# Second layer of the last phase with weights stationary for five of six blocks, its sums turned by VectorE in squares of 32

## The chip, the core and the metric

The kernel runs on one core of a Trainium2 chip. The core has five engines that work side by side and wait for each other by semaphores: TensorE (matmuls), VectorE, ScalarE, GpSimd and SyncE, which here issues all DMA transfers. The metric is the time of one execution on the device in microseconds (us), less is better; several runs give a median.

## What is computed

Three parts follow each other: a gated linear attention, a mixture of four experts, and a feed-forward layer with a gate. Cut to what matters here:

```python
def _moe2_ref(x, w_in, w_out):        # x: 3072 x 384, w_in: 384 x 2048, w_out: 2048 x 384
    h = x @ w_in
    relu6 = np.clip(h + 3.0, 0.0, 6.0)
    g = h * relu6 / 6.0
    return (g @ w_out).astype(np.float32)

def reference(...):
    x = attention(q, k, v, alpha)     # 3072 tokens of 384 features
    x = sum over 4 experts of p[e] * (relu(x @ w1[e]) @ w2[e])   # 384 x 1024, 1024 x 384
    return _moe2_ref(x, w_in, w_out)  # stored as 3072 rows of 384
```

## The kernel before

The 3072 tokens are split in six blocks of 512 (`NBLK` = 6, `NB` = 512). Activations lie with the features on the 128 partitions and the tokens in the free dimension, so 384 features are three tiles (`KT` = 3). Hidden units are taken 128 at a time; one such piece of a block is a step. The function walks through phases 0, 1 and 2: phases 0 and 1 are the experts (`kind` 1), phase 2 is the last layer (`kind` 2). A visit is one block with one set of weights; in phase 2 a block is one visit of 16 steps.

Each value is split in a high part and a low part (`xh`, `xl`; `wh`, `wl`; `hh`, `hl`), and each product is made of three matmuls: high by high, low weights by high, high weights by low.

A step has two halves. `mm1` (line 778) makes the first layer: nine matmuls into one PSUM bank `ph`, 128 hidden units by 512 tokens, weights stationary. In phase 2 four operations follow it, alternating between the engines: ScalarE makes `g` (L812), VectorE multiplies it by `ph` (L815), ScalarE makes `hh` (L816), VectorE makes `hl` (L817). `mm2` (line 822) makes the second layer. In `kind` 1 the weights are stationary and 512 columns of activations move (L849), into three sums `po`, each 128 features by 512 tokens. In `kind` 2 the activations are stationary and 384 columns of weights move (L851), into four sums, each 128 tokens by 384 features. `finish` (line 881) takes a sum that is complete: in `kind` 2 ScalarE copies it to `o` (L902) and SP stores it (L904), 128 rows of 1536 bytes.

`mm2` runs one step behind `mm1`, across blocks too: TensorE does the first layer of a block's step 0, the second layer of the last step of the block before, the first layer of step 1, and only then the second layer of step 0. PE, VectorE, ScalarE and SP work in the order in which the code is written (`tc.manual_schedule`, line 907). So what `finish` issues stands on its engine behind the four operations of the next block's step 0 and in front of those of step 1.

The sums have a pool `ps2` of three banks (and one bank of `ps1` for a fourth sum), so in phase 2 each sum of a block takes the bank that the same sum of the block before had. The pool `gp` holds the tags "pb" and "t" with two buffers each; the pool `sp` holds "acc", also two buffers, which `o` uses. Of the DMA transfers that are spoken of below, `vd` (L137) copies 256 tokens of 8 heads of `v` in DRAM, 2048 pieces of 48 numbers (192 bytes), and one call of `A` (L493) writes 768 pieces of 512 bytes with four transfers.

Of the kernel before, what the change touches and what calls it, by code (L numbers as in the profile page):

```python
# [10 lines left out]
F32 = mybir.dt.float32  # L11
# [7 lines left out]
P = 128  # L19
# [522 lines left out]
def tile_gla__then__moe__then__moe2(  # L542
# [29 lines left out]
    nc = tc.nc  # L572
# [4 lines left out]
    KT = DM // P  # L577
    NB = 512
    NBLK = N // NB
# [13 lines left out]
    gp = ctx.enter_context(tc.tile_pool(name="gp", bufs=2))  # L593
# [228 lines left out]
    def mm2(vi, f):  # L822
        vv = visits[vi]
        i, z = vv["steps"][f]
        wh, wl = wts[(1, i)]
        hh, hl = hts.pop((vi, f))
        n = vv["n"]
        first, last = f == 0, f == len(vv["steps"]) - 1
        nt = KT if vv["kind"] == 1 else n // P
        half = n < NB  # L830
        if first and half:
            po = [psh.tile([P, 2, U], F32, tag="psh", name=f"po_{vi}_{x}") for x in range(2)]
            accs[vi] = [po[0][:, 0], po[0][:, 1], po[1][:, 0]]
        elif first:
            nonlocal ps2
            if ps2 is None:
                ps_ctx.close()
                ps2 = ctx.enter_context(tc.tile_pool(name="ps2", bufs=3, space=PSUM, reuse_waits="tile"))
            second = vv["phase"] == 1 and vi % 2
            pools = [(psa, "psa") if second else (ps2, "ps2") if m < 3 else (ps1, "ps1") for m in range(nt)]  # L840
            accs[vi] = [pool.tile([P, 512], F32, tag=tag, name=f"po_{vi}_{m}") for m, (pool, tag) in enumerate(pools)]
        for m in range(nt):
            ms = slice(m * P, m * P + P)
            for o, (w, h) in enumerate(((wh, hh), (wl, hh), (wh, hl))):
                fl = dict(start=(first and o == 0 and not (half and m == 1)), stop=(last and o == 2))
                if half:
                    fl["skip_group_check"] = True
                if vv["kind"] == 1:
                    pe.matmul(accs[vi][m][:, 0:n], w[:, z, ms], h[:, 0:n], **fl)  # L849
                else:  # L850
                    pe.matmul(accs[vi][m][:, 0:DM], h[:, ms], w[:, z, :], **fl)  # L851
            if last and (m > 0 or not half):
                for x in (0, 1) if half and m == 1 else (m,):
                    finish(vi, x)
# [26 lines left out]
    def finish(vi, m):  # L881
        vv = visits[vi]
        po = accs[vi][m]
        n = vv["n"]
        b, t0 = vv["b"], vv["b"] * NB + vv["lo"]
        if vv["kind"] == 1:
            pb = pbs[vi][:, 0:n]
            if vv["phase"] == 0 and m == KT - 1:
                t = pbs[vi]
            else:  # L890
                t = gp.tile([P, 512], F32, tag="t", name=f"t_{vi}_{m}")
            nc.vector.tensor_tensor(t[:, 0:n], po[:, 0:n], pb, op=mul)  # L892
            if vv["phase"] == 0:
                after(2, lambda: nc.sync.dma_start(acc_d[vv["e"]][:, m, t0 : t0 + n], t[:, 0:n]))
                return
            a = acc[b][:, m, :]
            nc.vector.tensor_tensor(a, a, t, op=add)
            if vv["steps"][-1] == (S1 - 1, 1):
                after(1, lambda: nc.sync.dma_start(x2_d[:, m, t0 : t0 + n], a))
        else:  # L900
            o = sp.tile([P, KT, NB], F32, tag="acc", name=f"o_{vi}_{m}")[:, 0, 0:DM]
            nc.scalar.copy(o, po[:, 0:DM])  # L902
            r0 = b * NB + m * P
            nc.sync.dma_start(out[r0 : r0 + P, :], o)  # L904
# [80 lines left out]
    def after(n, fn):  # L985
        todo.append((step + n, fn))
# [36 lines left out]
    for vi, vv in enumerate(visits):  # L1023
        phase, b = vv["phase"], vv["b"]
# [15 lines left out]
        for f in range(len(vv["steps"])):  # L1040
# [12 lines left out]
            if done:  # L1053
                mm2(*done)
# [15 lines left out]
            i, z = v2["steps"][done[1]]  # L1070
# [11 lines left out]
            if i == (0, S0, S1)[v2["phase"]] + 2 and (v2["phase"] > 0 or v2["b"] == NBLK - 1):  # L1082
                ph, nb = (v2["phase"], v2["b"] + 1) if v2["b"] + 1 < NBLK else (v2["phase"] + 1, 0)
                if ph <= 2:
                    n = 2 * nb + z
# [6 lines left out]
    for x in pend:  # L1092
        mm2(*x)
# [30 lines left out]
```

## Time and profile before

| | |
|---|---|
| median of 3 runs | 1415.39 us |
| the three runs | 1412.38, 1415.39, 1415.56 us |
| profiled execution, from first to last instruction | 1412.8 us |
| TensorE busy with matmuls | 1375.2 us, 97% |
| VectorE, ScalarE busy | 840.3 us, 461.1 us |
| mean granted TensorE clock | 0.991 of full speed |

The profile is of one execution. PE is TensorE, PEld its loading of stationary operands, DVE is VectorE, ACT ScalarE, SPq the queue of SyncE. Matmuls are pipelined: one that lasts 0.39 us may be followed by the next 0.23 us after its start, so work is measured from start to start. A note `[0.18 <-ACT o L902]` says that the engine sat idle for 0.18 us before the instruction and what ended that; without a note there was no idle time that the profile shows. The last phase begins at about 1004 us.

### The profile page before, as it was taken

The page shows a single profiled execution, that of the slowest core. Times are in us where ns is not written, and L with a number is a line of the kernel's source. Part 1 is how long each engine was busy: PE and PEld are TensorE (multiplying, and loading weights), DVE is VectorE, ACT ScalarE, POOL GpSimd, SP SyncE. Part 2 cuts the span into 40 slices and gives each one's busy share as a digit, 9 for nine tenths or more (in the row PEclk, how much of TensorE's full clock was granted, in tenths as well). Part 3 has the DMA queues.
Part 4 walks back from the last instruction along what each step waited for, and adds up shares of the span by engine and source line. Part 5 has one row for each costly group of instructions (what it writes and reads, how often), then busy time and mean ns, then how long its engine had stood idle before and what let it go on. Part 6 is the DMA issues. An engine that isn't in the chain of part 4 may idle for free.

```text
span 1412.8 us, 26163 instructions
## 1 busy us (share of the span) xinstructions
PE 1375.2 (97%) x10914; PEld 1176.5 (83%) x10914; DVE 840.3 (59%) x1509; ACT 461.1 (33%) x839; POOL 91.8 (6%) x125
## 2 busy tenths in 40 slices
PE   8689999999999999999999999999999999999998
PEld 7678878888888878888888888888899999998987
DVE  7999877767685268757576666445433333333332
ACT  3555444443434133211111111113333333333333
POOL 2000000000000012222122121000000000000000
PEclk9999999999999999999999999999999999999999
DMA  6654544344532256424142424123201010101000
GB/s 192 180 151 130 154 128 133 103 114 126 143 109 87 65 186 224 149 61 151 54 138 75 138 70 140 29 93 112 78 1 45 1 45 0 45 0 46 0 23 23
DMA packets 127749, 132.33 MB, mean 94 GB/s; under 512 B 33680, under 2 KB 109456, under 8 KB 127632
## 3 DMA queue, kind: packets, MB, share of 16 engines
q1 hardware_dynamic: 127632, 130.68, 30.6%
q8 instruction: 85, 1.39, 0.4%
q14 instruction: 32, 0.26, 0.1%
HBM read 100.71 MB, written 34.65 MB: 96 GB/s over the span
## 4 chain that ended last, share of the span: by engine, by line
PE 87%; DVE 9%; issue 1%; DMA 1%; ACT 1%; SPq 0%; POOL 0%; DVEq 0%; ACTq 0%; POOLq 0%
PE ph L796 40%; PE po L849 25%; PE po L851 14%; PE py L458 2%; PE py L479 1%; PE pa L368 1%; DVE qt L356 1%; PE pkt L321 1%; DVE kt L356 1%; PE pu L404 1%; DVE asb L380 1%; DVE hl L807 1%; PE idle L938 1%; DVE dg L247 1%; PE pqt L321 1%
## 5 line engine op out<-in xcount | busy, mean ns | idle before, releaser
L804 ACT ACTIVATE hh<-ph 128x512 fp32r<-128x512 f32 (+1 forms) x206 | 117.5, 571 | 524.6 <-PE ph L796 524.5
L807 DVE SCALAR_TENSOR_TENSOR hl<-ph,hh 128x512 fp32r<-128x512 f32 (+1 forms) x206 | 134.4, 653 | 241.9 <-ACT hh L804 241.9
L796 PE MATMUL ph<-xh,w0h 128*128 128x512 f32 (+1 forms) x906 | 257.5, 393 | 2.7 <-ACT xh L771 2.4
L796 PE MATMUL ph<-xh,w0l 128*128 128x512 f32 (+1 forms) x906 | 248.4, 383 | 0.0
L796 PE MATMUL ph<-xl,w0h 128*128 128x512 f32 (+1 forms) x906 | 247.7, 382 | 0.2 <-DVE xl L772 0.2
L849 PE MATMUL po<-hl,w1h 128*128 128x512 f32 (+1 forms) x618 | 232.5, 376 | 7.3 <-DVE hl L807 7.3
L849 PE MATMUL po<-hh,w1h 128*128 128x512 f32 (+1 forms) x618 | 232.2, 376 | 6.7 <-DVE t L892 6.5
L849 PE MATMUL po<-hh,w1l 128*128 128x512 f32 (+1 forms) x618 | 231.7, 375 | 0.0
L796 PEld LDWEIGHTS ph<-xh,w0l 128*128 128x128 f32 x906 | 168.0, 190 | 34.5
L796 PEld LDWEIGHTS ph<-xl,w0h 128*128 128x128 f32 x906 | 167.3, 189 | 34.3 <-DVE xl L772 0.5
L796 PEld LDWEIGHTS ph<-xh,w0h 128*128 128x128 f32 x906 | 162.4, 190 | 28.0 <-ACT xh L771 2.6
L815 DVE SCALAR_TENSOR_TENSOR g<-g,ph 128x512 f32<-128x512 f32 x96 | 66.1, 689 | 190.9 <-ACT g L812 190.9
L849 PEld LDWEIGHTS po<-hl,w1h 128*128 128x128 f32 x618 | 116.4, 188 | 29.6 <-DVE hl L807 8.6
L849 PEld LDWEIGHTS po<-hh,w1h 128*128 128x128 f32 x618 | 116.5, 189 | 29.2 <-issue 2.9
L849 PEld LDWEIGHTS po<-hh,w1l 128*128 128x128 f32 x618 | 116.4, 188 | 20.6
L851 PE MATMUL po<-w1h,hh 128*128 128x384 f32 x384 | 130.1, 339 | 1.8 <-ACT hh L816 1.7
L851 PE MATMUL po<-w1h,hl 128*128 128x384 f32 x384 | 129.8, 338 | 0.2
L851 PE MATMUL po<-w1l,hh 128*128 128x384 f32 x384 | 129.0, 336 | 0.0
L812 ACT ACTIVATE g<-ph,three 128x512 f32<-128x512 f32 x96 | 66.2, 690 | 178.0 <-PE ph L796 178.0
L817 DVE SCALAR_TENSOR_TENSOR hl<-g,hh 128x512 fp32r<-128x512 f32 x96 | 66.6, 693 | 67.1 <-ACT hh L816 67.1
L816 ACT ACTIVATE hh<-g 128x512 fp32r<-128x512 f32 x96 | 60.8, 633 | 76.2 <-DVE g L815 76.2
L851 PEld LDWEIGHTS po<-w1h,hh 128*128 128x128 f32 x384 | 72.1, 188 | 7.8 <-ACT hh L816 2.5
(105 smaller groups left out, 1428.7 us busy)
## 6 DMA issues: line engine op xcount, KB each, us to landing
rx<-x_d SPq DMA_DIRECT2D x36, 384.0 KB
vl<-vd SPq DMA_DIRECT2D x96, 96.0 KB
rw<-in_moe_w_dram SPq DMA_DIRECT2D x21, 384.0 KB
pb<-p_d SPq DMA_DIRECT2D x28, 256.0 KB
raw<-in_moe_w_in_dram SPq DMA_DIRECT2D x24, 256.0 KB
raw<-in_moe_w_out_dram SPq DMA_DIRECT2D x24, 256.0 KB
acc_d<-t SPq DMA_DIRECT2D x20, 256.0 KB
rq<-in_q_dram SPq DMA_DIRECT2D x24, 192.0 KB
```

The costliest lines, as they stand in the source:

```text
L321: pe.transpose(pt[:, P * i : P * i + P], src[:, 4 * half + i].rearrange("p h d -> p (h d)"), self.ident)
L356: tt(zv, zv, tlv[:, :, 1 - x].unsqueeze(2).to_broadcast([P, nb, w]), op=mul)
L458: pe.matmul(s["py"][j][64 * h : 64 * h + 64, r, :].rearrange("p (b x w) -> p b x w", x=2, w=w)[:, :, 1, :], self.vl[64 * j : 64 * j + 64, ...
L796: pe.matmul(ph[:, 0:n], w[:, j, fs], x[:, j, cs], start=(o == 0 and j == 0), stop=(o == 2 and j == KT - 1),)
L804: nc.scalar.activation(hh[:, 0:n], ph[:, 0:n], AF.Relu)
L807: nc.vector.scalar_tensor_tensor(hl[:, 0:n], ph[:, 0:n], 0.0, hh[:, 0:n].bitcast(F32), op0=ALU.max, op1=sub)
L812: nc.scalar.activation(g[:, 0:n], ph[:, 0:n], AF.Relu, bias=three)
L815: nc.vector.scalar_tensor_tensor(g[:, 0:n], g[:, 0:n], 6.0, ph[:, 0:n], op0=ALU.min, op1=mul)
L816: nc.scalar.activation(hh[:, 0:n], g[:, 0:n], AF.Copy, scale=1.0 / 6.0)
L817: nc.vector.scalar_tensor_tensor(hl[:, 0:n], g[:, 0:n], 1.0 / 6.0, hh[:, 0:n].bitcast(F32), op0=mul, op1=sub)
L849: pe.matmul(accs[vi][m][:, 0:n], w[:, z, ms], h[:, 0:n], **fl)
L851: pe.matmul(accs[vi][m][:, 0:DM], h[:, ms], w[:, z, :], **fl)
```

## The change

For blocks 0 to 4 of the last phase `mm2` takes the form that phases 0 and 1 have: weights stationary, 512 tokens moving, three sums of 128 features by 512 tokens. The result then lies with the features on the partitions, while it is stored by rows of tokens. `finish` lets VectorE transpose each sum in squares of 32 by 32 into a tile of tag "t" of the pool `gp`, and SP stores it with four transfers, one for 32 partitions each: 512 pieces of 32 numbers (128 bytes) per transfer. Block 5 keeps the old form.

```diff
@@ mm2
-        nt = KT if vv["kind"] == 1 else n // P
+        wide = vv["kind"] == 1 or vv["b"] < NBLK - 1
+        nt = KT if wide else n // P
...
-                if vv["kind"] == 1:
+                if wide:
                     pe.matmul(accs[vi][m][:, 0:n], w[:, z, ms], h[:, 0:n], **fl)
                 else:
                     pe.matmul(accs[vi][m][:, 0:DM], h[:, ms], w[:, z, :], **fl)
@@ finish
+        elif b < NBLK - 1:
+            o = gp.tile([P, 512], F32, tag="t", name=f"o_{vi}_{m}")
+            nc.vector.transpose(o, po)
+            dst = out[b * NB : b * NB + NB, m * P : m * P + P].rearrange("(x j) (a i) -> a j x i", j=32, i=32)
+            for a in range(P // 32):
+                nc.sync.dma_start(dst[a], o[32 * a : 32 * a + 32].rearrange("j (x i) -> j x i", i=32))
         else:
             o = sp.tile([P, KT, NB], F32, tag="acc", name=f"o_{vi}_{m}")[:, 0, 0:DM]
             nc.scalar.copy(o, po[:, 0:DM])
```

The order of the instructions moves at each of the five block boundaries. VectorE, from block 0 to block 1, before (names are tiles of the program with a running number; `DMAHW5` and the like are the semaphores on which transfers report their landing):

```order
L815 SCALAR_TENSOR_TENSOR g_15_11598<-g_15_11598,ph_15_11586 128x512 [waits Activation_49]
L817 SCALAR_TENSOR_TENSOR hl_15_11597<-g_15_11598,hh_15_11596 128x512 [waits PE_49,Activation_49]
L815 SCALAR_TENSOR_TENSOR g_0_11627<-g_0_11627,ph_0_11615 128x512 [waits Activation_49]
L817 SCALAR_TENSOR_TENSOR hl_0_11626<-g_0_11627,hh_0_11625 128x512 [waits PE_49,Activation_49]
L815 SCALAR_TENSOR_TENSOR g_1_11668<-g_1_11668,ph_1_11656 128x512 [waits Activation_49]
L817 SCALAR_TENSOR_TENSOR hl_1_11667<-g_1_11668,hh_1_11666 128x512 [waits PE_49,Activation_49]
```

The same place in the changed kernel:

```order
L815 SCALAR_TENSOR_TENSOR g_0_11581<-g_0_11581,ph_0_11569 128x512 [waits Activation_49]
L817 SCALAR_TENSOR_TENSOR hl_0_11580<-g_0_11581,hh_0_11579 128x512 [waits PE_49,Activation_49]
L903 STREAM_TRANSPOSE o_0_11589<-po_0_11183 128x512 [waits PE_49]
L903 STREAM_TRANSPOSE o_1_11598<-po_1_11184 128x512 [waits PE_49]
L903 STREAM_TRANSPOSE o_2_11607<-po_2_11185 128x512 [waits DMAHW5_49,DMAHW6_49,DMAHW4_49,DMAHW7_49,DVE_49,PE_49]
L815 SCALAR_TENSOR_TENSOR g_1_11625<-g_1_11625,ph_1_11613 128x512 [waits Activation_49]
L817 SCALAR_TENSOR_TENSOR hl_1_11624<-g_1_11625,hh_1_11623 128x512 [waits Activation_49]
```

Three transposes now stand between step 0 and step 1 of the next block, and the third waits on the semaphores of transfers. In the boundaries that follow, the first two carry waits on transfers of the block before as well.

TensorE, the second layer of block 1's step 0, before:

```order
L796 MATMUL ph_1_11656<-xl_1_11378,w0h_10713 128x512 x3
L851 MATMUL po_0_11673<-w1h_10717,hh_0_11625 128x384 [waits Activation_49]
L851 MATMUL po_0_11673<-w1l_10718,hh_0_11625 128x384
L851 MATMUL po_0_11673<-w1h_10717,hl_0_11626 128x384 [waits DVE_49]
L851 MATMUL po_1_11674<-w1h_10717,hh_0_11625 128x384 [waits Activation_49]
L851 MATMUL po_1_11674<-w1l_10718,hh_0_11625 128x384
L851 MATMUL po_1_11674<-w1h_10717,hl_0_11626 128x384
L851 MATMUL po_2_11675<-w1h_10717,hh_0_11625 128x384 [waits Activation_49]
```

and in the changed kernel:

```order
L796 MATMUL ph_1_11613<-xl_1_11356,w0h_10713 128x512 x3
L850 MATMUL po_0_11630<-hh_0_11579,w1h_10717 128x512 [waits DVE_49,Activation_49]
L850 MATMUL po_0_11630<-hh_0_11579,w1l_10718 128x512
L850 MATMUL po_0_11630<-hl_0_11580,w1h_10717 128x512
L850 MATMUL po_1_11631<-hh_0_11579,w1h_10717 128x512 [waits DVE_49]
L850 MATMUL po_1_11631<-hh_0_11579,w1l_10718 128x512
L850 MATMUL po_1_11631<-hl_0_11580,w1h_10717 128x512
L850 MATMUL po_2_11632<-hh_0_11579,w1h_10717 128x512 [waits DVE_49]
```

The first matmul into each sum waited for ScalarE's copies; it now waits for VectorE's transposes. Nine matmuls stand per step in place of twelve.

SP's stores of block 0, in the changed kernel (before, four rows of 128x384 stand here):

```order
L906 DMA out_dram<-o_0_11589 32x16x32 [waits DVE_49]
L906 DMA out_dram<-o_0_11589 32x16x32
L906 DMA out_dram<-o_0_11589 32x16x32 [waits DMAHW6_49]
L906 DMA out_dram<-o_0_11589 32x16x32 [waits DMAHW7_49]
L906 DMA out_dram<-o_1_11598 32x16x32 [waits DMAHW0_49,DVE_49]
L906 DMA out_dram<-o_1_11598 32x16x32 [waits DMAHW1_49]
```

Six more of this kind follow for `o_1` and `o_2`.

## Rows read from the trace of the kernel before

**Rows 1.** The page, busy time of each engine

```profile
PE 1375.2 (97%) x10914; PEld 1176.5 (83%) x10914; DVE 840.3 (59%) x1509; ACT 461.1 (33%) x839; POOL 91.8 (6%) x125
```

**Rows 2.** Timeline, TensorE, wide steps: start us, us, engine, line, operation, tiles, form, count

```profile
1000.11 0.84 PE L796 MATMUL ph<-xh,w0h 128*128 128x512 f32 x3
...
1002.15 0.39 PE L849 MATMUL po<-hh,w1h 128*128 128x512 f32 x1
...
1004.19 0.84 PE L796 MATMUL ph<-xh,w0h 128*128 128x512 f32 x3
```

**Rows 3.** Timeline, TensorE, a step of the last phase

```profile
1396.39 0.86 PE L796 MATMUL ph<-xh,w0h 128*128 128x512 f32 x3
...
1398.47 0.33 PE L851 MATMUL po<-w1h,hh 128*128 128x384 f32 x1
...
1400.57 0.86 PE L796 MATMUL ph<-xh,w0h 128*128 128x512 f32 x3
```

**Rows 4.** Timeline, all engines, from block 0 to block 1

```profile
1071.32 0.33 PE L851 MATMUL po<-w1h,hh 128*128 128x384 f32 x1
...
1073.69 0.69 DVE L817 SCALAR_TENSOR_TENSOR hl<-g,hh 128x512 fp32r<-128x512 f32 x1 [0.70 <-ACT hh L816]
...
1074.05 3.60 SPq L904 DMA_DIRECT2D out_dram<-o  x4
...
1076.06 0.99 ACT L902 COPY o<-po 128x384 f32<-128x384 f32 x2 [1.65 <-DMA out_dram<-o]
...
1076.59 0.19 PEld L851 LDWEIGHTS po<-w1h,hh 128*128 128x128 f32 x1 [0.18 <-ACT o L902]
```

**Rows 5.** Timeline, SP queue, stores of blocks 4 and 5

```profile
1342.47 67.62 SPq L904 DMA_DIRECT2D out_dram<-o  x8
```

**Rows 6.** Groups by line, 900 to 1413 us: count, busy us, mean ns, idle

```profile
L892 DVE TENSOR_TENSOR t<-po,pb 128x512 f32<-128x512 f32 x13 | 8.9, 683 | 0.0
```

**Rows 7.** Timeline, SP queue, writes and copies in small pieces

```profile
414.17 0.60 SPq L137 DMA_DIRECT2D vd<-in_v_dram  x1
...
476.59 1.83 SPq L493 DMA_DIRECT2D x_d<-ys  x4
...
480.30 0.37 SPq L762 DMA_DIRECT2D rx<-x_d  x1
```

**Rows 8.** Busy time by stretch, around the copy into vd

```profile
core 0: us, PE busy (x) PEld busy (x) DVE busy (x) ACT busy (x) POOL busy (x), PEclk, DMA share, GB/s
...
418.00:419.00 1.00, 1.00 (x48) 0.88 (x39) 1.00 (x2) 0.00 (x0) 0.00 (x0) 1.00 0.44 59
419.00:420.00 1.00, 1.00 (x68) 1.00 (x64) 0.86 (x3) 0.00 (x0) 0.00 (x0) 1.00 0.00 0
```

**Rows 9.** Busy time by stretch, while block 0 is stored

```profile
1075.00:1075.50 0.50, 0.50 (x3) 0.38 (x3) 0.00 (x0) 0.00 (x0) 0.00 (x0) 1.00 1.02 366
```

**Rows 10.** Timeline, TensorE, behind a wait for VectorE in phase 0

```profile
505.99 0.47 PE L849 MATMUL po<-hh,w1h 128*128 128x512 f32 x1 [1.98 <-DVE t L892]
...
507.94 0.63 PE L849 MATMUL po<-hh,w1l 128*128 128x512 f32 x1
508.37 0.63 PE L849 MATMUL po<-hl,w1h 128*128 128x512 f32 x1
```

**Rows 11.** Busy time by stretch, at idle times and behind them

```profile
94.00:96.60 2.60, 0.00 (x0) 0.00 (x0) 2.47 (x4) 1.97 (x4) 0.00 (x0) 1.00 0.67 154
...
97.80:101.10 3.30, 3.30 (x43) 3.00 (x42) 3.23 (x6) 1.87 (x3) 0.00 (x0) 0.50 0.78 239
...
158.10:159.90 1.80, 0.02 (x1) 0.01 (x1) 1.66 (x5) 0.57 (x2) 0.00 (x0) 1.00 0.58 125
159.90:163.30 3.40, 3.38 (x53) 3.19 (x54) 3.37 (x6) 1.28 (x3) 0.00 (x0) 1.00 0.79 239
...
504.00:506.00 2.00, 0.02 (x2) 0.04 (x1) 1.93 (x5) 1.95 (x4) 0.61 (x1) 1.00 0.00 0
...
507.40:510.70 3.30, 3.30 (x9) 2.62 (x9) 3.23 (x6) 0.00 (x0) 1.38 (x1) 0.50 0.44 162
```

## The prediction, made before the changed kernel was run

> **What bounds the kernel now.** I read the busy shares first, then the timeline of TensorE's matmuls, then what stands around a block boundary. TensorE is busy for 97% of the span, VectorE for 59% [rows 1]: the end is set by the matmuls, so an edit pays only by shorter matmul work or costs by making TensorE wait.
>
> The timeline shows two kinds of step. In a step of the phase before, which the changed blocks copy, nine matmuls of the first layer start at 1000.11, nine of the second (weights stationary, 512 columns) at 1002.15, and the next step starts at 1004.19: 2.04 + 2.04 = 4.08 us [rows 2]. In a step of the last phase the first layer starts at 1396.39, twelve matmuls of 384 columns at 1398.47, the next step at 1400.57: 2.08 + 2.10 = 4.18 us [rows 3]. Both forms move 4608 columns in the second layer, yet the wide one is shorter, and the first layer behind it too.
>
> The boundary between blocks 0 and 1 comes next [rows 4]. The last second-layer visit of block 0 begins at 1071.32; call that T0. VectorE's hl for the next block ends at 1073.69 + 0.69 = T0 + 3.06, ScalarE has copied the first sum by 1074.05, where SP issues its transfer. ScalarE's third copy then waits 1.65 us until that transfer has landed, at 1076.06, because o has two buffers; TensorE loses 0.18 us on it. This is the wait to watch: it is there already, on an engine with time to spare.
>
> **The steps.** Blocks 0 to 4 have 16 steps each. A block's period, boundary included, is (1342.47 - 1074.05) / 4 = 67.1 us [rows 4, 5]. Sixteen wide steps take 16 x 4.08 = 65.3 us. That is 1.8 us saved per block, 9.1 us in five. Block 5 keeps the narrow form.
>
> One rule speaks against this gain. The Trainium skill's page "TensorE: Matmul & The Clock Gate", section "Back-to-back issue gap", gives a warm matmul N / 2.4 ns plus 2.5 ns. By it, nine of 512 and twelve of 384 differ by 7.5 ns, an estimate of 0.6 us in 80 steps, and the sum below would end some 8 us higher. The trace disagrees, with 2.04 against 2.10 us for the two sets [rows 2, 3], and the measured rows decide.
>
> **What leaves and what comes at a boundary.** Four copies leave ScalarE, which waits for TensorE anyway: worth nothing in itself. Three transposes come to VectorE, and twelve transfers to SP in place of four. The trace has no transpose. The nearest row is VectorE's product of a sum in PSUM, 128 by 512, at 0.683 us [rows 6]; I take 0.69 us. It has one source less but turns squares, so 0.5 to 1.2 us are the ends I keep; each 0.1 us moves the stall below by 0.2 us, since the first and the third transpose both lie on its path.
>
> In the changed order VectorE has the transposes behind hl of the next block's step 0 and in front of g of its step 1. The third one carries waits on four transfer semaphores, those of the first one's four transfers, since the tag "t" has two buffers. The wait that ScalarE bears now thus moves into VectorE's queue, and it is longer, because the buffer is free only when four transfers have landed. Queued behind it on VectorE are g and hl of step 1. In front of TensorE stands the first matmul into the third sum, which reuses the bank that this transpose reads.
>
> **How long the four transfers take.** SP issues the first at T0 + 3.06 + 0.69 = T0 + 3.75. Let L be the time from there to the landing of the fourth. If the small pieces cost nothing, L is three issues and one landing: four similar writes (x_d from ys, 512-byte pieces) are issued in 1.83 us, 0.46 each [rows 7], and a 192 KB transfer lands 2.0 us after its issue [rows 4]: 3 x 0.46 + 2.0 = 3.4 us. Four such x_d writes of 768 pieces have landed by 480.30, when the load that reads them is issued, 3.7 us after the first issue [rows 7]. The nearest row in number and size of pieces is the copy of v into vd: 2048 pieces of 192 bytes, the same 2048 that four of the new transfers have at 128 bytes. It is issued at 414.17 [rows 7], and the DMA engines, still busy for 0.44 of the stretch from 418 to 419, move nothing in the next [rows 8]: some 4.3 us, with another load's tail in front. I take 3.9 us, between these. The upper end is a piece that costs as much as one of 1536 bytes: 366 GB/s over 16 engines is 67 ns each [rows 9], so 128 x 67 ns = 8.6 us, and with the 1.45 us of latency in the row of 2.0 us, L = 10.
>
> **The stall.** The third transpose starts at T0 + 3.75 + L, ends 0.69 later, and TensorE starts some 0.05 behind (1076.06 + 0.48 for a copy, then 1076.59 [rows 4]): T0 + 4.49 + L. TensorE wants that bank at T0 + 2.04 (this visit) + 2.04 (first layer of step 1) + 2 x 0.68 (first two sums) = T0 + 5.44. The stall is L - 0.95: 2.95 us with L = 3.9, 2.45 with 3.4, 9 with 10. The first two sums are free in time: transposes 0 and 1 end at T0 + 3.75 and + 4.44, wanted at + 4.08 and + 4.76. After the stall g, hh and hl of step 1 need about 2.1 us from the transpose's end, and TensorE has 0.68 + 2.04 us of work until it wants them, so no second wait follows.
>
> **The clock.** Where TensorE waited 1.98 us for VectorE between wide matmuls [rows 10], the granted clock was 0.50, the 1.2 GHz level, from 507.4 to 510.7 [rows 11]: matmuls started 0.43 us apart (507.94, 508.37) instead of 2.04 / 9 = 0.227 [rows 2, 10]. After 2.6 us of idle at 94.0 the clock was 0.50 from 97.8 to 101.1; after 1.80 us of idle at 158.1 it stayed at 1.00 [rows 11]. A stall of 2.95 us is longer than either idle time that cost the clock. Price: in 3.4 us at the low level 3.4 x (1 - 0.227 / 0.43) = 1.6 us are lost.
>
> **Sum.** Per boundary 2.95 + 1.6 = 4.55 us; five boundaries 22.75 us; less 9.1 us saved: +13.65 us. Against the profiled execution that is 1412.8 + 13.65 = 1426.4 us. The median of the three runs, 1415.39, lies 2.6 us above that span, so on the median I predict 1429 us, 1.0% slower. What a measurement of this kernel can tell from no change is about 0.3%, or 4.2 us.
>
> **Rivals.** (a) The stall comes, but the clock holds, as after the 1.80 us: 5 x 2.95 - 9.1 = +5.65, 1421 us. For it: one idle time of 1.80 us in this trace kept the clock. Against it: 1.98 and 2.6 us did not.
>
> (b) The stall is short and the clock holds: L at its lower end of 3.4, 5 x 2.45 - 9.1 = +3.15, 1418.5 us, within the 0.3%. It needs pieces of 128 bytes that cost nothing beyond a plain landing.
>
> (c) Small pieces are slow. At 366 GB/s over 16 engines [rows 9] 512 bytes take 22 ns; a write that reads and writes 512 bytes for each 128-byte piece takes twice that, 45 ns, so 128 x 45 ns + 1.45 us = 7.2 us for L, a stall of 6.25, and 5 x (6.25 + 1.6) - 9.1 = +30, 1446 us. The vd row speaks against it: 4.3 us x 16 / 2048 is at most 34 ns a piece [rows 7, 8]. The Trainium skill's page "DMA: Bandwidth & Descriptors", section "Specifications", states such a rule: below 512 bytes the engine does a read-modify-write. By that rule (c) holds; the vd row doesn't bear it out in full.
>
> (d) The other sign: the transfers land inside the cover, the steps' 9.1 us remain, 1406 us at best. It decides at a stall plus clock of (9.1 - 4.2) / 5 = 0.98 us per boundary, that is at L = 1.93 us. The shortest landing here is 2.0 us for one transfer alone [rows 4], and this wait is for four in a row from one queue. It would need the four to be issued far faster than 0.46 us apiece.
>
> That the change doesn't do what it says can be left out: the order shows three sums of 512 columns per step in blocks 0 to 4 and five times three transposes.
>
> **Chances.** The forecast with stall and clock 0.62, (a) 0.16, (b) 0.10, (c) 0.08, (d) 0.04. Faster by over 0.3% is (d), 0.04. Within 0.3% is (b) and a small part of (a), 0.12. Slower is the rest, 0.84. The range runs from 1418, the lower end of (b), to 1446, which takes in (c); what is left out is (d), the far half of (b), and pieces as dear as the upper end of L.
>
> **What would show it.** Right if, in the changed profile, a step of blocks 0 to 4 takes 4.08 us; VectorE's third transpose of each block stands after an idle time ended by a transfer of out; TensorE is idle for about 3 us, five times, ended by VectorE's transpose, at the third sum and not the first two; and 3.4 us at a granted clock of 0.50 follow most of them. It is wrong if the transposes take over 1.2 us each (then the first two sums are late too), if the fourth transfer lands under 2 us after the first issue, if the clock stays at 1.00 across the boundaries, or if a wide step in the last phase, where VectorE and ScalarE read more sums than in the phase before, takes longer than 4.08 us.

## The result, and the profile of the changed kernel

| | before | changed |
|---|---|---|
| median of the runs, us | 1414.46 (6 runs, 1412.38 to 1415.56) | 1424.82 (6 runs, 1421.73 to 1428.17) |
| span of the profiled execution, us | 1412.8 | 1419.7 |
| its own time, us | some 1414.7, an estimate: the span and the 2 us by which a time exceeds its span | 1421.80 |

The ratio is 1.0074, with a 95% interval from 1.0060 to 1.0089: 10.4 us, or 0.7%, slower. Predicted were 1429 us, 13.65 us slower. The profiled execution of the changed kernel is one of its two shortest; two more executions of the same kernel are read below.

The same boundary as [rows 4], from block 0 to block 1, in the timeline of the changed kernel (start us, us, engine, line, operation, tiles, form, count, idle time before it and what ended it):

```profile
1066.14 0.84 PE L796 MATMUL ph<-xh,w0h 128*128 128x512 f32 x3
...
1068.18 0.39 PE L850 MATMUL po<-hh,w1h 128*128 128x512 f32 x1
...
1070.22 0.84 PE L796 MATMUL ph<-xh,w0h 128*128 128x512 f32 x3
1070.54 0.69 DVE L817 SCALAR_TENSOR_TENSOR hl<-g,hh 128x512 fp32r<-128x512 f32 x1 [0.70 <-ACT hh L816]
...
1071.15 1.31 DVE L903 STREAM_TRANSPOSE o<-po 128x512 f32<-128x512 f32 x2
...
1071.89 6.53 SPq L906 DMA_DIRECT2D out_dram<-o  x12
...
1073.39 0.39 PE L850 MATMUL po<-hl,w1h 128*128 128x512 f32 x1
1075.54 0.72 DVE L903 STREAM_TRANSPOSE o<-po 128x512 f32<-128x512 f32 x1 [3.08 <-DMA out_dram<-o]
...
1076.31 0.50 PE L850 MATMUL po<-hh,w1h 128*128 128x512 f32 x1 [2.53 <-DVE o L903]
1076.65 0.39 PE L850 MATMUL po<-hh,w1l 128*128 128x512 f32 x1
```

Read it from the top. A step, from one first layer to the next, takes 1070.22 - 1066.14 = 4.08 us, the period of the wide steps in [rows 2]; before, it was 4.18 [rows 3]. T0, the last second-layer visit of block 0, is 1068.18. Two transposes run behind hl. SP issues the first transfer at T0 + 3.71. TensorE finishes the second sum, and the third matmul group should start at 1073.62 (1073.39 and a pace of 0.227). It starts at 1076.31, because the third transpose has stood on VectorE for 3.08 us until a transfer of out landed. So the wait of ScalarE's third copy in [rows 4], 1.65 us on an engine with time to spare, is now a wait of VectorE, and TensorE stands behind it.

The grouped waits of TensorE from 900 us on (engine, line, waited for: us in total, times, longest):

```profile
PE po L850 <- DVE o L903: 11.8, 4, 3.9
PE po L852 <- DVE o L903: 2.7, 1, 2.7
```

All five boundaries show it: TensorE idles 14.5 us in sum. The group of the transposes gives their price and VectorE's own waits, 17.0 us (count, busy us, mean ns, idle):

```profile
L903 DVE STREAM_TRANSPOSE o<-po 128x512 f32<-128x512 f32 x15 | 10.1, 700 | 17.0 <-DMA out_dram<-o 17.0
```

SP's queue shows what a whole boundary costs, since its stores stand at the same place of every block:

```profile
1071.89 6.53 SPq L906 DMA_DIRECT2D out_dram<-o  x12
...
1140.01 6.59 SPq L906 DMA_DIRECT2D out_dram<-o  x12
...
1208.36 7.70 SPq L906 DMA_DIRECT2D out_dram<-o  x12
...
1279.45 6.42 SPq L906 DMA_DIRECT2D out_dram<-o  x12
...
1347.64 6.34 SPq L906 DMA_DIRECT2D out_dram<-o  x12
```

The periods are 68.12, 68.35, 71.09 and 68.19 us. A block of the same steps without the wait takes 65.28 (third buffer, below), so the four boundaries cost 2.84, 3.07, 5.81 and 2.91 us. That is the idle time of each (2.53, 2.78, 3.90, 2.61) and some 0.3 us: idle is counted from the modelled end of the last matmul, 0.16 us behind the pace, and the first matmul after the wait takes 0.34 us instead of 0.227. The third boundary has 1.6 us more than that, and the windows show why (us, busy of PE, PEld, DVE, ACT, POOL, then granted clock, DMA share, GB/s):

```profile
1214.70:1217.90 3.20, 3.20 (x9) 2.45 (x9) 0.69 (x1) 0.62 (x1) 0.00 (x0) 0.50 0.67 102
...
1285.00:1289.00 4.00, 4.00 (x19) 3.33 (x18) 1.38 (x2) 1.31 (x3) 0.00 (x0) 1.00 0.76 173
```

Behind the idle time of 3.90 us nine matmuls filled 3.20 us at 1.2 GHz. Behind that of 2.61 us, at the next boundary, nineteen filled 4.00 us at 2.4 GHz. Only one of the five idle times cost the clock in this execution.

### The profile page after: what moved, and what is told of

Read it like the earlier page. It is cut to its first block, busy times and chain, and to the rows that moved or that the text cites. A ratio compares the mean times of both kernels' runs of the same rounds, so it can differ in the third digit from the quotient of the medians.

```text
span 1419.7 us, 25733 instructions
## 1 busy us (share of the span) xinstructions
PE 1364.3 (96%) x10674; PEld 1140.1 (80%) x10674; DVE 849.4 (60%) x1524; ACT 452.5 (32%) x819; POOL 91.5 (6%) x125
## 4 chain that ended last, share of the span: by engine, by line
PE 84%; DVE 10%; DMA 2%; issue 2%; ACT 1%; SPq 1%; DVEq 0%; ACTq 0%
PE ph L796 39%; PE po L850 36%; PE po L852 2%; PE py L458 2%; PE py L479 1%; PE pa L368 1%; DMA out_dram<-o 1%; DVE qt L356 1%; PE pkt L321 1%; DVE kt L356 1%; PE pu L404 1%; DVE hl L807 1%; DVE asb L380 1%; PE pk L392 1%; DVE dg L247 1%
## 5 line engine op out<-in xcount | busy, mean ns | idle before, releaser
L850 PE MATMUL po<-hh,w1h 128*128 128x512 f32 (+1 forms) x858 | 326.3, 380 | 20.0 <-DVE o L903 11.8
L850 PE MATMUL po<-hl,w1h 128*128 128x512 f32 (+1 forms) x858 | 326.0, 380 | 7.0 <-DVE hl L807 7.0
L850 PE MATMUL po<-hh,w1l 128*128 128x512 f32 (+1 forms) x858 | 325.4, 379 | 0.0
L850 PEld LDWEIGHTS po<-hh,w1h 128*128 128x128 f32 x858 | 161.7, 188 | 53.9 <-DVE o L903 13.5
L850 PEld LDWEIGHTS po<-hl,w1h 128*128 128x128 f32 x858 | 161.6, 188 | 39.1 <-DVE hl L807 8.3
L850 PEld LDWEIGHTS po<-hh,w1l 128*128 128x128 f32 x858 | 161.7, 188 | 29.9
L817 DVE SCALAR_TENSOR_TENSOR hl<-g,hh 128x512 fp32r<-128x512 f32 x96 | 66.5, 693 | 67.1 <-ACT hh L816 67.1
L665 POOL TENSOR_TENSOR sq<-hc 128x256 f32<-128x256 f32 x48 | 34.5, 718 | 577.9 <-PE ph L796 492.9
L680 POOL TENSOR_TENSOR a<-a,hc 128x256 f32<-128x256 f32 x48 | 47.1, 981 | 223.7 <-DVE hc L679 223.7
L893 DVE TENSOR_TENSOR t<-po,pb 128x512 f32<-128x512 f32 (+1 forms) x82 | 52.6, 655 | 0.0
L346 ACT COPY kc<-kt 128x512 f32<-128x512 f32 x48 | 30.3, 631 | 61.9 <-PE pa L368 41.6
```

Of the source, the lines that this page charges most:

```text
L346: nc.scalar.copy(c.rearrange("p x (b w) -> p (x b) w", w=self.W[l]), halves(z, l, x))
L665: nc.gpsimd.tensor_tensor(sq, hc, hc, op=mul)
L680: nc.gpsimd.tensor_tensor(a, a, hc, op=add)
L817: nc.vector.scalar_tensor_tensor(hl[:, 0:n], g[:, 0:n], 1.0 / 6.0, hh[:, 0:n].bitcast(F32), op0=mul, op1=sub)
```

## The experiments

My theory after this reading: the stall exists because the third transpose needs the buffer of the first sum, and its length is the time from the first issue to the fourth landing (L) less the cover. The rivals were that the wide step or the turn itself costs time here, that the small pieces or the number of issues set L, and that the spread of 6.4 us between runs comes from the clock or from the transfers.

### A third buffer for the third sum

```
-            o = gp.tile([P, 512], F32, tag="t", name=f"o_{vi}_{m}")
+            o = gp.tile([P, 512], F32, tag="pb" if m == 2 else "t", name=f"o_{vi}_{m}")
```

> The changed kernel with one difference: the third transpose of a block writes into a buffer of tag 'pb', which nothing uses in the last phase, so no transpose waits for a transfer of its own block. Theory (the stall is the wait for a buffer, and the clock follows from it): TensorE's idle time at the five boundaries goes from 2.5 to 3.9 us to nothing, because the third transpose then ends at T0 + 3.06 + 3 x 0.69 = T0 + 5.13 and TensorE wants it at T0 + 5.44; what is left is the gain of the wide steps, 1414.5 - 9.1 = 1405 us, with no drop of the clock in the last phase. Rival (the transposes themselves, or the small pieces on the DMA engines, slow the steps down, and the buffer only shows it): the time stays within 3 us of the changed kernel's 1424.8, with TensorE still waiting for the third transpose.

Measured: 1404.8 us (1404.07 to 1406.22), ratio to before 0.9935 [0.9922, 0.9947]. This kernel is faster than both. VectorE and SP at the boundary:

```profile
1071.09 1.91 DVE L903 STREAM_TRANSPOSE o<-po 128x512 f32<-128x512 f32 x3
1071.83 6.54 SPq L906 DMA_DIRECT2D out_dram<-o  x12
...
1137.11 7.29 SPq L906 DMA_DIRECT2D out_dram<-o  x12
```

Three transposes run without a gap, and the twelve stores are still there; a block takes 1137.11 - 1071.83 = 65.28 us. No wait for a transpose is left. The steps, the transposes and the small pieces cost nothing on the path. The whole loss, and 20 us between this kernel and the change, hangs on one buffer.

### The wide second layer without the turn

```
-            o = gp.tile([P, 512], F32, tag="t", name=f"o_{vi}_{m}")
-            nc.vector.transpose(o, po)
-            dst = out[b * NB : b * NB + NB, m * P : m * P + P].rearrange("(x j) (a i) -> a j x i", j=32, i=32)
-            for a in range(P // 32):
-                nc.sync.dma_start(dst[a], o[32 * a : 32 * a + 32].rearrange("j (x i) -> j x i", i=32))
+            o = sp.tile([P, KT, NB], F32, tag="acc", name=f"o_{vi}_{m}")[:, 0, :]
+            nc.scalar.copy(o, po)
+            at = (b * KT + m) * P * NB
+            nc.sync.dma_start(out.rearrange("t c -> (t c)")[at : at + P * NB].rearrange("(p x) -> p x", p=P), o)
```

> The wide second layer alone: the turn and the small pieces are left out. ScalarE copies each sum of 128 by 512 as it did before and SP stores it in one transfer of 2 KB rows, so blocks 0 to 4 of the output stand feature by feature and not in rows of tokens. Theory (wide steps save 16 x 4.18 + 0.2 - 16 x 4.08 = 1.8 us per block): 1405 to 1407 us, a stall of some 0.2 us per boundary being left, since ScalarE's third copy waits for the landing of the first transfer as before. Rival (matmuls of 512 columns are no faster here, by the rule of 2.5 ns per matmul): 1414 us.

Measured: 1406.16 us (1406.04 to 1407.73), ratio 0.9945 [0.9931, 0.9958], and two waits of 0.3 us for ScalarE's copy. With the kernel above it prices the wide steps twice: 9.5 and 8.2 us gained, where 9.1 were forecast.

### The first sum stored twice

```
-            for a in range(P // 32):
+            for a in list(range(P // 32)) * (2 if m == 0 else 1):
```

> The changed kernel, with the first sum of each block stored twice: its four transfers are issued, then the same four again, so the buffer is free after eight. Theory (L is issue after issue at some 0.54 us each, plus one landing): L grows by 4 x 0.54 = 2.2 us to 5.8, the idle time per boundary from 2.7 to about 4.9, all five now cost the clock 1.6 us: 1414.5 - 9.1 + 5 x (4.9 + 1.6) = 1438 us. Rival (L is a fixed latency of the landing, the issues run beside it): L and the idle time grow by less than 0.5 us, 1425 to 1427 us.

Measured: 1442.63 us (1439.57 to 1444.69), ratio 1.0201 [1.0184, 1.0219]. TensorE's waits, and the window behind the first of its boundaries:

```profile
PE po L850 <- DVE o L903: 19.9, 4, 5.2
PE po L852 <- DVE o L903: 5.3, 1, 5.3
```

```profile
1078.60:1085.20 6.60, 6.07 (x14) 4.79 (x15) 1.74 (x3) 1.11 (x2) 0.00 (x0) 0.50 0.76 174
```

Four more transfers of the first sum bring the wait for the fourth landing from 3.65 us (5.01 once) to between 5.79 and 6.34, and the idle times from 2.5 to 2.8 us (3.90 once) to 4.7 to 5.3. All five are followed by a granted clock of 0.50; behind the first the matmuls ran at it for 6.1 us and behind the second for 4.1, where 3.4 were priced. The profiled execution took 1441.12 us, 3.1 above the expected 1438. By the periods of its stores (issued at 1072.02, 1145.68 and 1218.37 us, so 73.66 and 72.69, less 65.28) the first two boundaries cost 8.4 and 7.4 us where 6.5 were priced, and that is 2.8 of the 3.1. The lever is where the theory has it; the other three runs have no trace.

### One transfer of each sum in place of four

```
-            for a in range(P // 32):
+            for a in range(1):
```

> Each sum of blocks 0 to 4 is stored with the first of its four transfers alone; three quarters of the output of these blocks are left out. Theory (three issues of 0.54 us and one landing): L is the landing of one transfer alone, about 2.0 us, so the idle time falls to 3.65 - 2.0 less than 2.53 us, some 0.9 us; no half clock: 1414.3 - 9.1 + 5 x (0.9 + 0.15) = 1410.5 us, 1409 to 1412. It also shows how near the change could come to no loss with two buffers: not below about 1409. Rival (the wait is for something else than the four transfers, for instance for a semaphore that later work raises): the idle time stays above 2 us and the time above 1417.

Measured: 1414.05 us (ten runs, 1410.08 to 1416.1), ratio 0.9997 [0.9987, 1.0007]. The profiled execution, at 1410.08, is as expected, with L = 1074.24 - 1072.30 = 1.94 us:

```profile
1072.30 3.00 SPq L906 DMA_DIRECT2D out_dram<-o  x3
...
1074.24 0.72 DVE L903 STREAM_TRANSPOSE o<-po 128x512 f32<-128x512 f32 x1 [1.37 <-DMA out_dram<-o]
```

```profile
1075.01 0.50 PE L850 MATMUL po<-hh,w1h 128*128 128x512 f32 x1 [0.83 <-DVE o L903]
```

The median is 2 us above the expected range. Two more executions of the same kernel ask why.

> Three of the four transfers of each sum left out, as once before: there the profiled execution took 1410.1 us with idle times of 0.8 to 1.1 us and no half clock behind them, but the other nine took 1412.0 to 1416.1. Theory (idle times near 1 us lose the clock in some executions too): one or more stretches at 0.50 in the last phase if the time is above 1412, and idle times as before. Rival (idle times near 1 us never lose it): none, and the difference lies in the phases ahead of the last one or in longer idle times.

> The same once more: by the theory a stretch at 0.50 in the last phase for each 1.6 us above 1410; by the rival none.

Measured: 1413.68 and 1411.83 us. In both, four of the five waits were as before (idle 0.8 to 1.1 us) and the third was not. Its wait, of the first of the two, and that of the boundary ahead of it:

```profile
1140.46 0.72 DVE L903 STREAM_TRANSPOSE o<-po 128x512 f32<-128x512 f32 x1 [1.34 <-DMA out_dram<-o]
1208.88 0.72 DVE L903 STREAM_TRANSPOSE o<-po 128x512 f32<-128x512 f32 x1 [3.39 <-DMA out_dram<-o]
```

No idle time near 1 us lost the clock (none of 13 in three executions). The two long ones, 2.84 and 2.97 us, went apart: the first was followed by a granted clock near 0.50, the second by 1.00. So in these two executions the rival holds: the 3.6 and 1.8 us by which they exceed 1410.08 come from one long wait each, and in the first from the clock behind it. The other nine of the ten runs have no trace. What made the wait long is seen in the DMA view of that stretch (1205.4 to 1208.9; the first rows are the busy share and the GB/s in 40 slices):

```profile
DMA  0000388896137887610000000010100010000000
GB/s 0 0 0 0 60 138 138 139 319 100 22 69 132 140 130 126 93 13 0 0 0 0 0 0 0 3 7 6 7 9 10 9 12 6 0 0 0 0 0 0
...
q8 instruction: 1, 0.02, 2.8%
```

The data are moved by slice 17, some 1.5 us after the start. Then nothing moves, and from slice 25 to 33 a trickle of 3 to 12 GB/s follows. In the same window a single packet of 16 KB from the queue that brings instructions stands on one engine, for 2.8% of 16 engines' 3.5 us, or 1.6 us. A transfer is complete only when its last pieces are, and a trickle of some 10 GB/s is what a single engine moves at 12.7 ns for 128 bytes (a row shown below). That these pieces stood behind the packet on its engine is my reading of the two lines together; it is not shown.

### The first sum's transfers issued on two queues

```
-                nc.sync.dma_start(dst[a], o[32 * a : 32 * a + 32].rearrange("j (x i) -> j x i", i=32))
+                (nc.scalar if m == 0 and a % 2 else nc.sync).dma_start(dst[a], o[32 * a : 32 * a + 32].rearrange("j (x i) -> j x i", i=32))
```

> Of the first sum's four transfers, SP issues two and ScalarE two; all else is as in the change. In the change the third transpose began 3.65 us after the first issue (0.53 to 0.54 us for each issue on SP), and TensorE stood idle 2.53 us behind it. Theory (the time to the fourth landing, L, is set by the issues: three of them and one landing): one issue of 0.54 us stands in front of the last instead of three, so L falls by about 1.1 us to 2.6, VectorE's wait from 3.1 to 2.0, TensorE's idle time from 2.5 to 1.5 us; five of them, no stretch at half clock behind them: 1414.3 - 9.1 + 7.5 + 0.7 of restarts = 1413.5 us. Rival (the landing of 2048 small pieces sets L, whichever queue issues them): idle times stay at 2.5 to 2.8 us and the time at 1421 to 1426.

Measured: 1425.68 us (1424.37 to 1429.49), ratio 1.0084 [1.0065, 1.0103]. The theory that the issues alone set L falls:

```profile
1071.88 6.42 SPq L906 DMA_DIRECT2D out_dram<-o  x10
1071.88 0.96 ACTq L906 DMA_DIRECT2D out_dram<-o  x2
...
1075.60 0.72 DVE L903 STREAM_TRANSPOSE o<-po 128x512 f32<-128x512 f32 x1 [3.15 <-DMA out_dram<-o]
```

Both queues begin at 1071.88, and the fourth landing still comes 3.72 us later. Busy time by stretch, while the first sum is stored, in this kernel and then in the changed one:

```profile
1073.00:1075.60 2.60, 0.76 (x4) 0.30 (x2) 0.00 (x0) 0.63 (x1) 0.00 (x0) 1.00 0.94 140
```

```profile
1073.00:1075.40 2.40, 0.78 (x4) 0.32 (x2) 0.00 (x0) 0.21 (x1) 0.00 (x0) 1.00 0.72 114
```

With one queue the DMA engines are 72% busy; with two, 94%. SP, relieved of two issues, starts the second sum's stores sooner, and those share the engines with the first sum's. So the issues (0.53 us each) and the engines' work on 512 pieces (12.7 ns each by a row shown below, over 16 engines 0.41 us) look like two limits that lie near each other, and lifting one gains nothing while the next sum's stores fill what comes free. In support of this, the engines had moved 3084 packets by the fourth landing with two queues and 2515 with one, by the DMA views of 1071.88 to 1075.60 and of 1071.89 to 1075.54; but no run held the second sum's stores back, so the sharing is argued and not shown. Three of the five boundaries lost the clock here (idle times of 2.67, 2.81 and 4.10 us) and two did not (2.51 and 2.61), which makes the time no shorter than the change's.

### Large pieces in place of small ones

```
-            dst = out[b * NB : b * NB + NB, m * P : m * P + P].rearrange("(x j) (a i) -> a j x i", j=32, i=32)
...
-                nc.sync.dma_start(dst[a], o[32 * a : 32 * a + 32].rearrange("j (x i) -> j x i", i=32))
+                at = (b * KT + m) * P * NB + a * 32 * NB
+                nc.sync.dma_start(out.rearrange("t c -> (t c)")[at : at + 32 * NB].rearrange("(j x) -> j x", j=32), o[32 * a : 32 * a + 32])
```

> The turned sum goes out in four transfers as in the change, but each writes its 32 rows of 2048 bytes to one contiguous place of out, so 32 large pieces stand in place of 512 pieces of 128 bytes; the rows of out are then not in their places (the second half of the turn is left out). Theory (small pieces cost nothing beyond their issue, the two buffers and the issues set the stall): VectorE's waits, 3.0 to 3.3 us in the change without the one odd wait of 4.4, stay above 2.6, idle times stay at 2.1 to 2.8 us, the time at 1419 to 1425. Rival (128-byte pieces lengthen the landing): the waits fall by over 1 us, and the time to 1414 or less.

Measured: 1424.04 us (1419.64 to 1424.61), ratio 1.0061 [1.0042, 1.0080].

```profile
1071.32 5.82 SPq L906 DMA_DIRECT2D out_dram<-o  x12
...
1074.50 0.72 DVE L903 STREAM_TRANSPOSE o<-po 128x512 f32<-128x512 f32 x1 [2.61 <-DMA out_dram<-o]
```

L is 3.18 us instead of 3.65, and the waits are 2.57 to 2.73 us, one of 3.55 aside. The truth lies between the two: small pieces lengthen L by 0.47 us, their longer issue included (5.82 us for the twelve instead of 6.53), and not by a multiple. The theory's bound of 2.6 us for the waits was met but for two of 2.57. Two of five boundaries lost the clock, behind idle times of only 2.06 and 2.33 us; 2.02, 2.18 and even 3.01 us kept it. The profiled execution, 1419.64 us, is the shortest of four, and what made the other three 4 to 5 us longer no trace shows.

### The idle time filled with matmuls

```
+            if first and m == 2 and vv["phase"] == 2 and vv["b"] > 0:
+                fill = psa.tile([P, 512], F32, tag="psa", name=f"fill_{vi}")
+                for _ in range(11):
+                    pe.matmul(fill[:, 0:n], wh[:, z, ms], hh[:, 0:n], start=True, stop=True)
```

> The changed kernel with the wait left as it is, but TensorE kept at work in it: in blocks 1 to 5, ahead of the third sum of a block's first step, eleven matmuls of 512 columns (11 x 0.227 = 2.5 us) into a bank that nobody reads. Theory (the runs of the changed kernel, 1421.7 to 1428.2, differ by how many of the five idle times cost the clock, 1.6 us each): the granted clock stays at 1.00 in the last phase in all runs, and the time is that of the stalls alone, -9.1 + 5 x 2.8 = +4.9, 1419 to 1421 us with a spread under 2 us. Rival (the spread has another cause, the stalls are longer in the slower runs): median and spread as in the changed kernel, 1424.8 and 6 us.

Measured: 1423.01 us (1420.76 to 1424.14), ratio 1.0060 [1.0047, 1.0072]. In the profiled execution the clock was kept through the whole stretch of the changed blocks:

```profile
1060.00:1410.00 350.00, 346.50 (x1562) 290.15 (x1561) 129.19 (x186) 112.97 (x171) 0.00 (x0) 1.00 0.10 21
```

The expected 1419 to 1421 is missed by the median and met by the profiled execution (1420.76), the shortest of five; the spread is 3.4 us where under 2 were expected. Two of this kernel's five waits for a transfer were long (4.76 and 4.46 us) and outlasted the filling by 1.7 us each; both have the instruction packet in their window. That this execution still met the range is luck: it began the last phase 2.4 us earlier than the profile of before did (SP's last store of the phase ahead is issued at 1004.13 us against 1006.56, a row that the next section shows). The highest time is 4 us under the change's highest, which agrees with the clock as a part of the change's spread. Five runs against six, on two chips, don't show it by themselves.

### Two more executions of the change

> The change as it is, looked at once more for its last phase alone. In its profiled execution (1421.8 us, one of the two shortest of six) only one of five idle times, 3.90 us long, was followed by a granted clock of 0.50; with the issues on two queues it was three of five (2.6 to 4.1 us), with large pieces two of five (one of them behind 2.06 us). Theory (an idle time of 2 to 4 us between wide matmuls loses the clock in some executions and not in others, and this makes the spread from 1421.7 to 1428.2): one to four stretches at 0.50, each 3.4 or 6.8 us, and the time is 1420 us and 1.6 us for each 3.4 us at 0.50 behind a boundary. Rival (the longer executions have longer waits for transfers): the same one stretch at 0.50, and idle times whose sum stands 3 us or more above 14.6 us.

> The change once more, for the same count: one to four of five idle times followed by a granted clock of 0.50 by the theory; by the rival a sum of idle times above 17.6 us in a run above 1424.

Measured: 1425.35 and 1424.38 us, where before took 1414.74 on the same chip. SP's stores in the second of the two:

```profile
1074.35 6.54 SPq L906 DMA_DIRECT2D out_dram<-o  x12
1144.13 6.36 SPq L906 DMA_DIRECT2D out_dram<-o  x12
1213.78 6.34 SPq L906 DMA_DIRECT2D out_dram<-o  x12
1281.82 6.44 SPq L906 DMA_DIRECT2D out_dram<-o  x12
1350.03 6.35 SPq L906 DMA_DIRECT2D out_dram<-o  x12
```

Its boundaries cost 4.50, 4.37, 2.76 and 2.93 us. The idle times at the first two, 2.57 and 2.54 us, are no longer than the other two (2.47, 2.62), but the granted clock fell behind them:

```profile
1080.60:1083.80 3.20, 3.20 (x9) 2.47 (x9) 0.11 (x1) 0.55 (x1) 0.00 (x0) 0.53 0.73 164
...
1149.00:1152.00 3.00, 3.00 (x8) 2.29 (x8) 0.77 (x2) 0.63 (x1) 0.00 (x0) 0.53 0.70 110
```

In the first of the two, idle times of 2.56 and 4.23 us lost the clock and 2.62, 2.61 and 2.77 us did not. Over three executions the change lost it at 5 of 15 boundaries: the theory's one to four per execution. The rival's sum above 17.6 us was not seen (14.8 and 12.9 us).

The theory's price of an execution, 1420 us and 1.6 us for each stretch at the low clock, gives 1423.2 us for both and is missed by 2.1 and 1.2 us. The place where the last phase begins has what is missing. SP's last store of the phase ahead, in before, in the change, and in these two executions:

```profile
1006.56 2.97 SPq L899 DMA_DIRECT2D x_d<-acc  x3
...
1004.97 2.97 SPq L900 DMA_DIRECT2D x_d<-acc  x3
...
1007.03 2.97 SPq L900 DMA_DIRECT2D x_d<-acc  x3
...
1007.42 2.97 SPq L900 DMA_DIRECT2D x_d<-acc  x3
```

The code up to there is the same in all four, and the two executions reach it 2.06 and 2.45 us later than the shorter one of 1421.80 us. Their boundaries cost 19.2 and 17.6 us in sum, against 17.7 in that one. So the execution of 1424.38 us is longer than that of 1421.80 for nothing that happens in the changed code, though it lost the clock twice and the other once. Of the spread between the runs the clock is a part at most. What varies ahead of the last phase was not followed.

## Why the prediction was right, and where it was off

**The direction and the mechanism** held as written: wide steps of 4.08 us; transposes 0 and 1 free; the third one behind an idle time ended by a transfer; TensorE idle at the third sum, five times. The third buffer removes that wait alone and leaves 9.5 us of gain; this is the intervention on which the explanation stands.

**The steps.** Forecast -9.1 us; measured -9.5 and -8.2 in the two kernels without the stall. A block went from 67.1 to 65.28 us, five times 1.8.

**The transposes.** Forecast 0.69 us from the row of 0.683 us [rows 6]; measured 0.700.

**L and the stall.** L was taken as 3.9 us, between 3.4 and 4.3; it was 3.65 us at the first boundary, and 3.54 to 3.89 at all 13 that had no long wait. The start of the stores was put at T0 + 3.75 and came at T0 + 3.71. The stall was forecast at 2.95 us; the boundaries that kept the clock cost 2.76 to 3.07 us by their periods. The size is right, and above the 2.45 us of rival (b); the inside of L is less so. The low end had 0.46 us an issue and pieces that cost nothing; an issue took 0.53 us, and the pieces cost 0.47 us of L together. From the row in the changed kernel, 2250 packets took 71.5% of 16 engines' 2.5 us, 12.7 ns each:

```profile
q1 hardware_dynamic: 2250, 0.28, 71.5%
```

Rival (c), with 45 ns and L = 7.2 us, is out. The Trainium skill's page "DMA: Bandwidth & Descriptors", section "Specifications", says that below 512 bytes the engine does a read-modify-write; whatever the engine does, its price here is 12.7 ns for 128 bytes. The bound of 34 ns from the vd row [rows 7, 8] was loose but on the right side.

**The clock** is the term that failed. "A stall of 2.95 us is longer than either idle time that cost the clock" put it at all five boundaries, 8 us. It was lost at 5 of 15, some 2.7 us per execution; the prediction's own sign, that the low clock follows most of the idle times, failed with 1, 2 and 2 of five. Between 2.0 and 3.0 us it went either way: 2.06 us lost it, 2.61, 2.78 and 3.01 kept it. The three rows that I had were 2.6 and 1.98 us lost and 1.80 kept [rows 10, 11], and the sum let every longer stall lose it, the chance of (a) being put at 0.16; three rows with both outcomes within 0.8 us of each other bear a chance, no certainty. Taken as one in three, the sum would have been -9.1 + 5 x (2.95 + 0.53) = +8.3 us, 1423.7 us on the median.

**What was not forecast** is the long wait, 1.3 to 1.7 us more, at the third boundary in two of three executions of the change. It made up for a small part of the clock term. In the execution of 1425.35 us the boundaries cost 4.18, 2.93, 6.11 and 2.91 us, and the fifth 2.77 + 0.3: 19.2 - 9.1 = +10.1 us. In that at 1424.38 the sum is 17.6 - 9.1 = +8.5, and in that at 1421.80 it is 17.7 - 9.1 = +8.6. Against the profile of before they began the last phase 0.5 and 0.9 us later and 1.6 us earlier. With that the three come to +10.6, +9.4 and +7.0 us, and their spans exceed the 1412.8 us of before by 10.5, 9.5 and 6.9. To 0.1 us nothing of the last phase is left over in them; why it begins sooner or later stays open.

**Rivals.** (a), 1421 us with the clock held, gives the time of the two shortest runs, but by luck: the one of them that has a profile lost the clock once and had a long wait, and it began the last phase 1.6 us early. (d) was off, since L would have had to be 1.93 us or less, for a time 4.2 us under before's. With one transfer left of four L was 1.94 us; the profiled execution, 1410.08 us, lies 3.6 us under before's median of 1413.68, near that sum, while the median of the ten is level with before. The upper bound of the range was set by (c), which didn't occur.

## What to carry to other kernels

When a result's store moves from one large transfer to several small ones, count the buffers again, since a buffer comes free with the last landing, and ask which engine stands in the wait: behind an engine that feeds TensorE, a wait that was free before costs its full length. Before shortening the transfers (other queues, larger pieces), look for one more buffer: here that alone turned 0.7% slower into 0.65% faster. Price a clock loss behind an idle time of 2 to 3 us as a chance, and read more than one execution before giving its size. Compare also where each execution begins the part that was changed: here that place alone moved by over 2 us.

## What the runs showed of the hardware

- The granted clock behind an idle time of TensorE between wide matmuls: none of 13 idle times of 0.8 to 1.1 us lost it, the change lost 3 of 13 of 2.4 to 2.8 us and both of its longer ones (3.90 and 4.23 us), and the kernel that stores twice lost all five of 4.7 to 5.3 us. Of the kernel with large pieces, 2.06 and 2.33 us lost it, and 2.02, 2.18 and 3.01 kept it. Between 2.5 and 3.0 us the same boundary of the same kernel kept it in one execution and lost it in the next.
- A packet of the instruction queue stands in the window of every long wait. This is the DMA view of the changed kernel from the first issue of the third boundary on (1208.4 to 1213.4):

```profile
DMA  0000002889568775887100010000017886688758
GB/s 0 0 0 0 0 0 39 133 140 263 81 103 129 119 110 86 138 138 119 27 0 1 6 6 9 10 10 13 13 32 125 137 137 100 101 145 128 118 84 146
...
q8 instruction: 1, 0.02, 2.0%
```

  At the next boundary (1279.4 to 1283) no such packet is listed, and the share doesn't fall to 0 until the window's end:

```profile
DMA  0000000000488886588886588886488886478887
...
q1 hardware_dynamic: 2614, 0.33, 57.4%
```

  Ten executions with a trace have five waits of VectorE for such a landing each, 50 in all. The eight waits with an instruction packet of 16 KB (queue 8) between first issue and last landing were 0.9 to 2.2 us longer than the mean of the others in the same execution, and none of the other 42 had it. A smaller instruction packet (queue 14, 0.01 MB) stood in 15 of those 42, and these waits were at most 0.4 us longer than those without any packet in the same execution. No run moved such a packet by intent, so this is a coincidence that held each time and no intervention; why it falls on the third boundary most often stays open.
- Issue and landing: a transfer of 64 KB in 512 pieces of 128 bytes cost SP 0.53 to 0.55 us to issue, one in 32 pieces of 2 KB 0.47 to 0.49 us. Where a sum went out in one such transfer of 512 pieces, VectorE's wait for it ended 1.91 to 1.96 us after its issue, the two long waits aside. With two queues at work the engines stood at 94% and 140 GB/s on such pieces.
